# K slots with one kvh per partition quadrant, V in 4-KB runs, one softmax pass for all heads, and P and q turned by VectorE

## Chip, cores, metric

One core of one Trainium2 chip. The time is device microseconds of one execution. It is given as a median with the range over several runs, with the kernel before run again on the same chip each time. A run more than 1.5% above the fastest of its kernel counts as slow.

Some words: a load (DMA) is split into packets, here one for each contiguous run of bytes, which the 16 DMA engines move. A packet lands when its data are written. The tail is the time from the last landing of K or V to the end. The granted clock is the share of its full clock that TensorE was given (1.0 is all). P is the softmax's output, and to turn is to transpose.

## The reference, cut to what matters

Eight decode rows (B = 8, one position each) pass through two rounds of attention (A) and a dense MLP with SiLU (B), with residuals:

```python
x = x + A(layernorm(x), k_cache, v_cache, wq, wo)   # 16 q heads, 8 kv heads, Dh = 256
x = x + B(layernorm(x), w1, w2)
x = x + A(...)      # same weights, same cache
x = x + B(...)
# A: W = 1024; k = k_cache[:, :, Sk-W:, :], v likewise (Sk = 4096);
#    softmax(q k^T / 16) v, each kv head (kvh) serves two q heads
```

The last 1,024 rows of K and V of all 8 batches and 8 kvh are 2 x 33.6 MB in bf16. Both rounds use them, so each batch's K and V stay on chip for both.

## The kernel before, cut to what the change touches

Each batch needs 8 slots for K and 8 for V, each of 128 partitions x 4,096 bytes; 30 slots take turns. SP issues all loads in order, and a load waits until its slot is free. VectorE transposes each K slot in place in 32 x 32 blocks of 4-byte elements. TensorE then takes the scores with q spread over a block-diagonal operand.

```python
def load_k(s, b, kvh):                    # one kvh per slot; 128 x 4,096 B on both sides
    dma(lambda e: e.dma_start(slots[s][:, :].rearrange("p (u d) -> p u d", d=DH),
                              A_k_cache[b, kvh, S0:SK, :].rearrange("(p u) d -> p u d", p=P)), ...)

def load_v(s, b, g):                      # runs of 1,024 B, in the order of P's transpose
    if g >= 4:
        dma(lambda e: e.dma_start(slots[s][:, :].rearrange("v (q n) -> v q n", q=4),
                  A_v_cache[b, g, S0:SK, :].rearrange("(q v uh) d -> v q (uh d)", q=4, uh=2)), ...)
        return
    ...

def softmax(b, layer, prio):              # two halves of four kvh each
    # transpose of the maxima, min, transpose back; then
    for k2 in range(2):
        act(... ACTF.Exp, bias=mb[ei][:, k2:k2 + 1] ...)
    pe([... ident, is_transpose=True ... for c in range(4)], ...)      # P turned by TensorE
    act(... pT_sb ... ACTF.Copy ...)

# q of round 2: a ScalarE copy out of PSUM, then TensorE matmuls turn it
seq = [(b, t, k) for b in range(NB) for t in "kv" for k in range(8)]   # order of the loads
```

## Time and profile before

| | before |
|---|---|
| time | 255.09 us median of 3 (253.25 to 255.13) |
| last packet of K or V lands at | 218.9 us of 255.3 |
| TensorE busy | 195.3 us (76%) |
| chain that ended last | TensorE 59%, SP's queue 16%, DMA 8% |
| median of a 4,096-byte packet | 161 ns |

The row that matters is the second. Until then the 16 DMA engines are busy all the time and pace the batches; after it comes a tail of 36.4 us of compute alone. The profile is of a run of 257.17 us, some 2 us longer than the median; its granted clock dips between 64 and 80 us.

### The profile page before, as it was taken

What the parts mean: (1) busy time and instruction counts of PE and PEld (TensorE: products, weight loads), DVE (VectorE), ACT (ScalarE), POOL (GpSimd) and SP (SyncE); (2) the same over time, 40 slices, a digit from 0 to 9 for tenths busy, and PEclk for the clock granted to TensorE, in tenths of its full rate; (3) what the DMA queues carried; (4) which work ended last, traced back from release to release, by engine and by line L of the source; (5) the groups of instructions that cost most, each with busy time, mean ns of one, the idle gap of its engine ahead of it and who ended that gap; (6) DMA issues with size and microseconds to landing.
All of it is one profiled execution on the core that took longest, in us unless ns stands there. A gap on an engine that the chain in (4) does not pass through costs nothing.

```text
span 255.3 us, 8598 instructions
## 1 busy us (share of the span) xinstructions
PE 195.3 (76%) x3820; PEld 105.1 (41%) x3820; DVE 153.3 (60%) x416; ACT 89.0 (35%) x241; POOL 11.8 (5%) x25
## 2 busy tenths in 40 slices
PE   0053211298869998998899899979988898998795
PEld 0051100043434556454544645444455255443452
DVE  6458665907842895597289559828954685302221
ACT  2002165714213442354343235334432433333211
POOL 1200000000000000000000000000000000000000
PEclk9999999999768999999999999999999899999999
DMA  6999999999999999999999999999999998200000
GB/s 236 361 395 379 309 342 347 352 362 404 369 349 393 372 335 311 392 388 347 362 411 362 338 373 400 350 363 403 372 334 388 379 325 265 75 3 3 0 3 5
DMA packets 50229, 78.23 MB, mean 306 GB/s; under 512 B 2304, under 2 KB 41104, under 8 KB 49808
## 3 DMA queue, kind: packets, MB, share of 16 engines
q1 hardware_dynamic: 50192, 77.68, 87.2%
q8 instruction: 30, 0.49, 0.8%
q14 instruction: 7, 0.06, 0.1%
HBM read 77.67 MB, written 0.01 MB: 304 GB/s over the span
## 4 chain that ended last, share of the span: by engine, by line
PE 59%; SPq 16%; DMA 8%; DVE 6%; ACT 6%; issue 3%; POOL 0%; ACTq 0%; DVEq 0%
PE bank L700 11%; PE bank L641 11%; DMA slot<-in_A_v_cache_dram 8%; PE bank L769 6%; SPq L481 6%; PE bank L817 6%; SPq L431 5%; PE bank L776 5%; ACT qbd L663 3%; PE bank L519 3%; PE bank L804 2%; DVE mseg L648 2%; PE bank L539 2%; SPq L469 2%; ACT qrow L824 2%
## 5 line engine op out<-in xcount | busy, mean ns | idle before, releaser
L946 DVE STREAM_TRANSPOSE slot<-slot 128x512 uint32<-128x512 uint32 x128 | 83.6, 689 | 6.2 <-DMA slot<-in_A_k_cache_dram 5.7
L700 PE MATMUL bank<-slot,pT_sb 128*2 128x256 bf16 x960 | 40.3, 282 | 13.4 <-DMA slot<-in_A_v_cache_dram 10.8
L641 PE MATMUL bank<-slot,qbd 128*8 128x256 bf16 x1024 | 40.7, 298 | 8.7 <-DVE slot L946 6.1
L641 PEld LDWEIGHTS bank<-slot,qbd 128*8 128x8 bf16 x1024 | 26.0, 89 | 15.5 <-DVE slot L946 6.7
L700 PEld LDWEIGHTS bank<-slot,pT_sb 128*2 128x2 bf16 x960 | 19.7, 83 | 24.3 <-issue 10.3
L663 ACT ACTIVATE qbd<-bank,mseg 128x256 bf16<-128x256 f32 x32 | 13.5, 470 | 34.9 <-DVE mseg L659 34.9
L648 DVE TENSOR_REDUCE mseg<-bank 128x1 f32<-128x256 f32 x32 | 13.2, 413 | 19.6 <-PE bank L641 19.3
L714 DVE TENSOR_TENSOR oT<-bank,l_sb 128x16 bf16<-128x16 f32 (+1 forms) x32 | 6.4, 199 | 27.6 <-PE bank L710 26.6
L776 PE MATMUL bank<-wq_sb,cols_b 128*128 128x512 bf16 x64 | 19.6, 388 | 0.0
L754 POOL TENSOR_TENSOR rhalf<-var,nhalf 128x1 f32<-128x1 f32 x16 | 8.8, 549 | 213.7 <-ACT var L752 213.7
L708 ACT ACTIVATE qbd<-bank 128x256 bf16<-128x256 f32 x32 | 12.2, 382 | 18.3 <-PE bank L700 18.3
L769 PE MATMUL bank<-wo_sb,oT 128*1 128x449 bf16 x256 | 17.7, 365 | 0.0
L610 ACT ACTIVATE qbd<-bank,mask 128x128 bf16<-128x128 f32 x32 | 12.1, 378 | 15.6 <-PE bank L605 14.3
L817 PE MATMUL bank<-wq_sb,xbt 128*1 128x512 bf16 x256 | 16.4, 378 | 0.6 <-DVE xbt L743 0.6
L783 PE MATMUL bank<-wq_sb,cols_b 128*128 128x512 bf16 x49 | 14.3, 402 | 0.0
L668 PE MATMUL bank<-ident,qbd 128*128 128x128 bf16 x64 | 6.8, 233 | 9.5 <-ACT qbd L663 8.8
L824 ACT ACTIVATE qrow<-bank 128x512 bf16<-128x512 f32 x16 | 9.5, 596 | 12.3 <-PE bank L817 12.0
L789 ACT ACTIVATE qrow<-bank 128x449 bf16<-128x449 f32 x8 | 4.4, 548 | 21.7 <-PE bank L769 21.7
L450 DVE TENSOR_REDUCE qbd<-wo_sb 128x5 f32<-128x2240 bf16 x4 | 9.7, 2481 | 2.8 <-DMA wo_sb<-in_A_wo_dram 2.8
L624 DVE TENSOR_TENSOR qbd<-bank,maskr 128x256 bf16<-128x256 f32 x16 | 6.8, 424 | 6.2 <-PE bank L619 6.1
L668 PEld LDWEIGHTS bank<-ident,qbd 128*128 128x128 bf16 x64 | 4.0, 103 | 13.6 <-ACT qbd L663 12.8
L710 PEld LDWEIGHTS bank<-ident,qbd 128*128 128x128 bf16 x64 | 3.7, 98 | 12.6 <-ACT qbd L708 6.8
(146 smaller groups left out, 214.9 us busy)
## 6 DMA issues: line engine op xcount, KB each, us to landing
slot<-in_A_k_cache_dram SPq DMA_DIRECT2D x64, 512.0 KB, 8.8
slot<-in_A_v_cache_dram SPq DMA_DIRECT2D x64, 512.0 KB, 8.2
wo_sb<-in_A_wo_dram SPq DMA_DIRECT2D x1, 3584.0 KB, 17.4
wq_sb<-in_A_wq_dram SPq DMA_DIRECT2D x3, 1024.0 KB, 6.8
w_sb<-in_B_w_dram SPq DMA_DIRECT2D x4, 336.0 KB, 15.9
w_sb<-in_B_w_dram SPq DMA_DIRECT2D x1, 1344.0 KB, 11.3
wq_sb<-in_A_wq_dram SPq DMA_DIRECT2D x2, 256.0 KB, 10.0
w_sb<-in_B_w_dram SPq DMA_DIRECT2D x4, 112.0 KB, 9.1
```

Of the source, the lines that this page charges most:

```text
L431: dma(lambda e, j=j: e.dma_start(rows[:, 3 * j:3 * j + 3, :], parts[j, 0:3 * P, :].rearrange("(c p) n -> p c n", p=P)), [("w2", j)], 3 * P ...
L481: dma(lambda e: e.dma_start(slots[s][:, :].rearrange("v (j n) -> v j n", j=4), src.rearrange("j (v uh) d -> v j (uh d)", uh=2)), [("slot", ...
L641: fns.append(lambda e, cb=cb, par=par, j=j, kvh=kvh, kv=kv: e.matmul(bank[sc][32 * j:32 * j + 8, k2 * 256:(k2 + 1) * 256], qbd[qi][:, kvh, ...
L648: dve(lambda e: e.tensor_reduce(mseg[layer][:, k2:k2 + 1], bank[sc][:, k2 * 256:(k2 + 1) * 256], AX.X, ALU.max, negate=True), bk(sc), [("m ...
L663: act(lambda e, k2=k2: e.activation(e_sb[ei][:, k2, :, :].rearrange("p uh (jj ul) -> p uh jj ul", ul=4), bank[sc][:, k2 * 256:(k2 + 1) * 2 ...
L700: fns.append(lambda e, q=q, uh=uh, j=j, vv=vv: e.matmul(bank[ob][32 * j:32 * j + 2, c0:c0 + DH], pT_sb[ei][:, k2 * 2 + uh, j * 8 + 2 * q:j ...
L769: fns.append(lambda e, i=i, c=c, kvh=kvh: e.matmul(bank[XB][32 * c:32 * c + 1, 0:D1], oT1[:, i % 2, i // 2:i // 2 + 1], wo_sb[:, i * DP:i ...
L776: pe([lambda e: e.matmul(bank[SC[1]][:], zero_b.broadcast_to([P, P]), wq_sb[:, 0:512], start=False, stop=True, skip_group_check=True) for ...
L783: pe(lambda e: e.matmul(bank[bi][:], zero_b.broadcast_to([P, P]), wq_sb[:, 0:512], start=False, stop=True, skip_group_check=True), [("wq", ...
L817: pe([lambda e, j=j, c=c, k2=k2, wb=wb: e.matmul(bank[wb][32 * j:32 * j + 1, :], xbt[:, xcol(c, k2):xcol(c, k2) + 1], wq_sb[:, c * HD + (( ...
L824: act(lambda e, wb=wb: e.activation(qrow[:], bank[wb][:], ACTF.Copy), bk(wb), ["rowb"], 0.55, prio, "qrow")
L946: dve(lambda e, v=v: e.transpose(v, v), [("slot", s)], [("slot", s)], 0.67, prio, "KT")
```

## The change

The intent: put four kvh into each K slot, one per quadrant of 32 partitions, so that the scores of all 16 heads of a slot come out of one group of matmuls and the softmax needs one pass. VectorE's 32 x 32 block transpose then turns P, and the keys of P's rows lie so that each V slot is one kvh in runs of 4,096 bytes. The block transpose also turns q of round 2.

```diff
-    def load_k(s, b, kvh):
-        dma(lambda e: e.dma_start(slots[s][:, :].rearrange("p (u d) -> p u d", d=DH),
-                                  A_k_cache[b, kvh, S0:SK, :].rearrange("(p u) d -> p u d", p=P)),
+    def load_k(s, b, i):
+        k2, g = i // 4, i % 4
+        src = A_k_cache[b, 4 * k2:4 * k2 + 4, S0 + 256 * g:S0 + 256 * g + 256, :]
+        dma(lambda e: e.dma_start(slots[s][:, :], src.rearrange("j (i u) d -> j i (u d)", u=8)),
-    def load_v(s, b, g):
-        ... (runs of 1,024 B)
+    def load_v(s, b, kvh):
+        dma(lambda e: e.dma_start(slots[s][:, :], A_v_cache[b, kvh, S0:SK, :].rearrange("(p u) d -> p (u d)", p=P)),
... softmax: two max, two transposes, min -> one max, one scale, one small matmul, one min
-        for k2 in range(2):
-            act(lambda e, k2=k2: e.activation(... ACTF.Exp, bias=mb[ei][:, k2:k2 + 1], scale=1.0),
-        pe([lambda e, c=c: e.matmul(... ident[:, :], is_transpose=True ...) for c in range(4)],
-        act(lambda e: e.activation(pT_sb[ei] ... ACTF.Copy),
+        act(lambda e: e.activation(e_t, bank[sc][:, 0:256], ACTF.Exp, bias=mb[ei][:, 0:1], scale=1.0),
+        dve(lambda e: e.transpose(p_t, e_t), ...)
... q of round 2
-            act(lambda e, wb=wb: e.activation(qrow[:], bank[wb][:], ACTF.Copy),
-            pe([... qturn ...]); dve(... qT2 ...); q_blocks(k2, prio)
+            dve(lambda e, wb=wb: e.transpose(bank[wb][:], bank[wb][:]), ...)
+            dve(... spread straight into qbd ...)
... (q of round 1 spread by GpSimd; tables of the scheduler, which set the order of the work, retuned)
```

## The prediction

> **What bounds the kernel now.** I read the page's slices first, then stretches of 4 us, then the waits and the chain that ended last. The slices:
>
> ```profile
> DMA  6999999999999999999999999999999998200000
> GB/s 236 361 395 379 309 342 347 352 362 404 369 349 393 372 335 311 392 388 347 362 411 362 338 373 400 350 363 403 372 334 388 379 325 265 75 3 3 0 3 5
> DMA packets 50229, 78.23 MB, mean 306 GB/s; under 512 B 2304, under 2 KB 41104, under 8 KB 49808
> ```
>
> The 16 DMA engines are 90% busy or more in nearly all of the first 33 slices (33 x 6.38 = 211 us) and idle afterwards. The rate swings although they are equally busy. Stretches of 4 us in batch 5 and one in the tail show why (columns: length, busy time and instructions of PE, weight load, VectorE, ScalarE, GpSimd, granted clock, DMA share, GB/s):
>
> ```profile
> 152.00:156.00 4.00, 4.00 (x72) 1.81 (x64) 3.72 (x8) 2.93 (x8) 0.55 (x1) 1.00 1.02 412
> 156.00:160.00 4.00, 4.00 (x94) 2.47 (x93) 3.91 (x10) 1.38 (x4) 0.00 (x0) 1.00 1.04 385
> 160.00:164.00 4.00, 3.93 (x72) 1.71 (x74) 3.37 (x8) 1.84 (x5) 0.55 (x1) 1.00 1.09 351
> 164.00:168.00 4.00, 3.29 (x95) 2.44 (x86) 1.82 (x7) 1.12 (x3) 0.00 (x0) 1.00 1.11 348
> 220.00:224.00 4.00, 4.00 (x77) 1.69 (x75) 1.65 (x10) 0.92 (x2) 0.00 (x0) 1.00 0.01 4
> ```
>
> K loads (4,096-byte packets) land at about 407 GB/s, V loads (1,024-byte packets) at about 349. A batch has 8 of each at 524,288 B: 4.19 MB / 407 = 10.3 us and 4.19 / 349 = 12.0 us, together 22.3 us. In the chain the first MLP matmuls of successive batches start at 132.14 and 154.63, a period of 22.5 us. So the middle of the run is DMA-bound; what remains is a tail of about 36 us, from the last V landing near 219 to 255.3, which runs on compute alone. The waits agree:
>
> ```profile
> PE bank L700 <- DMA slot<-in_A_v_cache_dram: 10.8, 7, 4.9
> ```
>
> TensorE loses 10.8 us to late V data, and 5.5 us of that kind stands in the chain in every second batch. Compute alone would need about 22.5 - 2.7 = 19.8 us per batch, close behind the DMA.
>
> **What the Trainium skill says.** "DMA: Bandwidth & Descriptors", section "Why a DMA increments its semaphore by 16 and not by 1": the number k of engines that a DMA uses is the largest one up to 16 that divides the sizes of both access patterns' slowest dimension that is not 1; on the SP queue it is the lowest-numbered k engines, and each adds one semaphore write. The trace agrees. The program has 145 DMAs, of which two (x and the output) have 8 rows: 143 x 16 + 2 x 8 = 2304, and the page counts 2304 packets under 512 B. All of these are 4-byte writes in the packet records. So the 8-row DMAs used 8 engines.
>
> The same page, "Why small descriptors are slow (HBM only)", gives a fixed cost per packet. The packet records agree: median 161 ns for 4,096 B, 48 ns for 1,024 B, 309 ns for 8,192 B. That is 10 ns plus 27.2 bytes per ns. Not one in a hundred of the 4,096-byte packets is under 159 ns, so one engine moves at most 25.7 GB/s.
>
> "SBUF — State Buffer", section "Door 1: The DMA port swizzle": partitions 0..63 reach only the 8 even ports, 64..127 only the odd ones. The trace agrees: among the first 160 packets of 4,096 B lie the 128 of the two 64-partition wq loads. Those 160 took 253 ns in the mean (median 270), the K packets after them 164.
>
> **The change part by part.**
>
> *K loads.* This decides the case. Before, source and destination were both 128 x 2,048, so k = 16. After, as built, the destination is 128 x 2,048 but the source is 4 x 32 x 2,048, the four kvh outermost. The largest k that divides 128 and 4 is 4. All 64 K loads then run on the same four engines, 32 packets of 4,096 B on each, where before it was 8 on each of 16. Load of each of these four engines, at the medians of before:
> - K: 64 x 32 = 2,048 packets x 0.161 = 329.7 us
> - V (one 4,096-byte run per partition, k = 16): 64 x 8 = 512 x 0.161 = 82.4 us
> - weights: 369 x 0.046 (896 B) + 24 x 0.140 + 24 x 0.309 + 8 x 0.075 + 8 x 0.27 = 30.6 us
>
> The sum is 443 us, against roughly 217 us per engine now. None of it lies beside anything that could hide it: compute needs under 20 us per batch, and these four engines need 41.2 + 10.3 = 51.5 us.
>
> *Port conflicts.* Engines 0 and 1 would write partitions 0..31 and 32..63, which share the even ports, and 2 and 3 share the odd ones; each walks through the 8 ports in the same order, four packets on each. In step, a packet would take 270 to 300 ns; more than four packets apart, 161. The four start in step. A few packets per engine in the trace take 0.4 to 1.3 us, and each shifts one engine by some packets, so I estimate that they fall apart within the first 30 to 50 us and then meet by chance. Two engines spread evenly over a cycle of 32 packets conflict for a quarter of it at half strength, +12%; V packets of the other twelve engines cross too. I put K at 0.193 us in the mean (estimate, +20%): 2,048 x 0.193 = 395 us, and the sum at 510 us.
>
> *V loads.* 32,768 packets of 1,024 B become 8,192 of 4,096 B. With K on 16 engines this alone would be 12.0 - 10.3 = 1.7 us per batch, 13.7 us in all. Against it, the first PV group now needs four V slots instead of one.
>
> *Softmax.* Per layer and batch: two maxima, two transposes and one more reduction become one maximum, one scale (about 0.17), one small matmul (0.2) and one reduction (0.16); two Exp become one; four transposing matmuls (0.40) and a ScalarE copy (0.28) become one VectorE transpose of 128x256. From the 512-column transposes (0.689) and the 32-column ones (0.212) I interpolate 0.43. From the last maximum to the first PV the chain shows 237.46 to 240.32 = 2.86 us; I get 2.4, about 0.5 saved.
>
> *q.* The rows that go are these, and the ScalarE copy is on the chain of layer 2:
>
> ```profile
> L824 ACT ACTIVATE qrow<-bank 128x512 bf16<-128x512 f32 x16 | 9.5, 596 | 12.3 <-PE bank L817 12.0
> L624 DVE TENSOR_TENSOR qbd<-bank,maskr 128x256 bf16<-128x256 f32 x16 | 6.8, 424 | 6.2 <-PE bank L619 6.1
> ```
>
> In the tail the chain runs from the first q matmul at 230.50 to the end of scores at 237.43. With a 0.7 us transpose in PSUM and a 0.2 us spread per half, and both q matmul groups back to back, I get 4.1 us: 2.8 saved. Layer-1 spreading moves from ScalarE (12.1 us) to idle GpSimd. VectorE gains 16 x 0.7 and 16 x 0.43 and loses about as much; at 153 us of 255 it has room, and a DMA that feeds it half as fast leaves it more.
>
> *Sum.* Start 2 + DMA 510 + tail 36.4 - 0.5 - 2.8 = 33: 545 us.
>
> **The rivals.**
> 1. K is spread over 16 engines after all. Then all loads run at 407 GB/s, 20.6 us per batch: 255 - 13.7 - 3.3 = 238 us, 7% faster, perhaps 240 to 245 if compute takes over the bound. For it: the change looks meant for that. Against it: the rule and the 2304.
> 2. Four engines without port conflicts: 2 + 443 + 33 = 478 us. For it: nothing holds the engines in step. This is nearly the floor, as 159 ns is the shortest usual packet.
> 3. Four engines in step throughout: K at 0.29 us gives 594 + 113 + 35 = 742 us. Against it: the long packets that shift single engines.
> 4. A wait for four V slots or the doubled VectorE transposes become the bound: a few us, hidden under the K loads.
>
> **Range and chances.** The mechanism rests on a rule whose trace evidence is exact, so I give it 94%. Within it the open size is the conflict: 478 without, 742 with it always. I take 545, and 468 to 680 as the range. Faster 5% (rival 1), the same 1%, slower 94%.
>
> **What would show each step right or wrong.** Right: packets under 512 B fall to 79 x 16 + 64 x 4 + 2 x 8 = 1536; mean rate near 78 / 0.545 = 143 GB/s; DMA digits of 3 to 5 instead of 9; K issue to landing tens of us instead of 8.8; VectorE's transposes wait for K loads, and PE's busy share falls below 45%. The packet records tell the conflict apart: the median of 4,096 B stays 161 to 165 with a tail near 300, or lies at 270 and more. Wrong: 2304 small packets, DMA at 9 throughout and 400 GB/s in V stretches as well, which is rival 1. The softmax and q steps can only be seen in the tail, as 33 against 36 us after the last V landing.

## The result, and the profile after

524.48 us median of 4 (523.06 to 525.66), against 255.11 (253.25 to 259.39) for the kernel before. The ratio is 2.061, 95% interval 2.048 to 2.074. The 259.39 counts as slow. Here and below a ratio is the one for the fast runs (here the means, 524.42 over 254.49), so not quite the ratio of the quoted medians.

The page of the kernel after: TensorE's busy time, then its slices and those of the DMA, and the packets.

```profile
PE 231.2 (44%) x3601; PEld 108.9 (21%) x3628; DVE 160.4 (31%) x404; ACT 60.0 (11%) x162; POOL 16.5 (3%) x41
PE   0201108250272338531764067333853176423988
DMA  7224995239422654247422933275423942284200
GB/s 285 99 104 140 270 370 221 100 117 238 139 104 104 194 155 156 103 146 201 160 105 105 231 132 138 105 181 159 161 103 129 216 159 98 104 200 140 99 1 4
DMA packets 24882, 78.19 MB, mean 150 GB/s; under 512 B 1536, under 2 KB 7568, under 8 KB 24464
```

Packets under 512 B fell from 2304 to exactly the 1536 that four engines per K load imply. The DMA digit is no longer 9 but swings between 2 and 9, and where it is 2 (two tenths of 16 engines) the rate is 98 to 105 GB/s. Stretches of 6 us of the same run (columns as in the prediction's table of stretches):

```profile
386.00:392.00 6.00, 4.53 (x44) 1.31 (x45) 1.84 (x5) 1.46 (x4) 0.55 (x1) 0.54 0.26 104
404.00:410.00 6.00, 0.00 (x0) 0.00 (x0) 1.30 (x2) 0.00 (x0) 0.00 (x0) 0.60 1.03 246
410.00:416.00 6.00, 0.00 (x0) 0.00 (x0) 0.00 (x0) 0.00 (x0) 0.00 (x0) 0.50 1.02 232
440.00:446.00 6.00, 3.54 (x45) 1.43 (x48) 1.54 (x3) 1.14 (x3) 0.13 (x1) 0.50 0.26 104
494.00:500.00 6.00, 5.58 (x101) 2.49 (x99) 0.79 (x5) 2.01 (x5) 0.55 (x1) 1.00 0.01 3
```

Three kinds of stretch: four engines alone (share 0.26, 104 GB/s, so 26 GB/s each); all 16 busy but only 232 to 246 GB/s, with every compute engine nearly idle; and the tail. The packet records say the same. For 287 us of the run about four packets are in flight, and a 4,096-byte one takes 163.6 ns in the mean. For 140 us at least 15 are in flight, and one takes 249 ns in the mean (median 268). The last packet of V lands at 490.0 us, and the tail is 33.0 us.

The waits of VectorE's K transposes, first of the kernel before, then of the kernel after (us in total, times, longest):

```profile
DVE slot L946 <- DMA slot<-in_A_k_cache_dram: 5.7, 4, 4.0
```

```profile
DVE slot L909 <- DMA slot<-in_A_k_cache_dram: 286.6, 64, 8.1
```

Before, 4 waits for K; after, 64 and 286.6 us. The wait for K now ends the chain too. The chain by engine, before and after, and three pieces of the chain after (start, us, what):

```profile
PE 59%; SPq 16%; DMA 8%; DVE 6%; ACT 6%; issue 3%; POOL 0%; ACTq 0%; DVEq 0%
```

```profile
DMA 53%; SPq 27%; PE 12%; DVE 5%; issue 2%; ACT 0%; ACTq 0%
...
391.66 29.65 DMA slot<-in_A_k_cache_dram
...
427.37 16.21 DMA slot<-in_A_k_cache_dram
...
449.67 30.22 DMA slot<-in_A_k_cache_dram
```

Each batch of the second half has one such pair, about 45 us of K that nothing hides. The granted TensorE clock fell as well (mean 0.739 against 0.973), but TensorE is 44% busy and in the tail, where it does bound, the clock is back at 1.0.

### The profile page after: what moved, and what is told of

Its sections match the earlier page's. It is cut to its first block, busy times and chain, and to the rows that moved or that the text cites. A ratio compares the mean times of both kernels' runs of the same rounds, so it can differ in the third digit from the quotient of the medians.

```text
span 523.0 us, 8141 instructions
## 1 busy us (share of the span) xinstructions
PE 231.2 (44%) x3601; PEld 108.9 (21%) x3628; DVE 160.4 (31%) x404; ACT 60.0 (11%) x162; POOL 16.5 (3%) x41
## 2 busy tenths in 40 slices
DMA packets 24882, 78.19 MB, mean 150 GB/s; under 512 B 1536, under 2 KB 7568, under 8 KB 24464
## 4 chain that ended last, share of the span: by engine, by line
DMA 53%; SPq 27%; PE 12%; DVE 5%; issue 2%; ACT 0%; ACTq 0%
DMA slot<-in_A_k_cache_dram 53%; SPq L475 14%; SPq L479 8%; SPq L435 3%; DVE slot L909 3%; PE bank L631 3%; PE bank L672 2%; PE bank L516 2%; PE bank L742 1%; PE bank L749 1%; DVE bank L791 1%; SPq L424 0%; PE bank L783 0%; PE bank L715 0%; PE bank L805 0%
## 5 line engine op out<-in xcount | busy, mean ns | idle before, releaser
L909 DVE STREAM_TRANSPOSE slot<-slot 128x512 uint32<-128x512 uint32 x128 | 86.4, 696 | 286.8 <-DMA slot<-in_A_k_cache_dram 286.6
L631 PE MATMUL bank<-slot,qbd 128*16 128x256 bf16 x1024 | 53.0, 376 | 97.6 <-DVE slot L909 45.8
L783 PE MATMUL bank<-wq_sb,xbt 128*1 128x512 bf16 x256 | 28.2, 584 | 100.7 <-DVE xbt L709 98.3
L631 PEld LDWEIGHTS bank<-slot,qbd 128*16 128x16 bf16 x1024 | 29.8, 114 | 125.2 <-DVE slot L909 47.5
L672 PE MATMUL bank<-slot,ep 128*2 128x256 bf16 x960 | 43.3, 302 | 12.8 <-DMA slot<-in_A_v_cache_dram 11.1
L672 PEld LDWEIGHTS bank<-slot,ep 128*2 128x2 bf16 x960 | 20.2, 85 | 28.6 <-issue 21.7
L677 ACT ACTIVATE ep<-bank 128x256 bf16<-128x256 f32 x32 | 12.3, 383 | 27.8 <-PE bank L672 25.8
L770 PE MATMUL bank<-w_sb,hT 128*1 128x449 bf16 x112 | 12.8, 551 | 2.7 <-DVE hT L767 2.7
L516 PE MATMUL bank<-w_sb,xbt 128*1 128x448 bf16 x128 | 11.8, 512 | 0.0
L791 DVE STREAM_TRANSPOSE bank<-bank 128x512 f32<-128x512 f32 x16 | 11.1, 694 | 1.2 <-PE bank L783 1.2
L454 DVE TENSOR_REDUCE ep<-wo_sb 128x5 f32<-128x2240 bf16 x4 | 9.7, 2479 | 4.0 <-DMA wo_sb<-in_A_wo_dram 4.0
L683 DVE TENSOR_TENSOR oT<-bank,l_sb 128x16 bf16<-128x16 f32 (+1 forms) x32 | 6.1, 190 | 14.5 <-PE bank L679 14.4
```

Source lines behind the costliest of these rows:

```text
L516: pe([lambda e, c=c, j=j: e.matmul(bank[XB][32 * j:32 * j + 1, 0:D], xbt[:, xcol(c, j // 2):xcol(c, j // 2) + 1], w1_r(j, c), start=(c == ...
L631: fns.append(lambda e, cb=cb, par=par, g=g, kv=kv: e.matmul(bank[sc][32 * g:32 * g + H, 0:256], qbd[qi][:, k2, cb * 2 + par, :], kv[:, cb, ...
L672: fns.append(lambda e, u=u, j=j, vv=vv, pt=pt: e.matmul(bank[ob][32 * j:32 * j + 2, c0:c0 + DH], pt, vv, start=(u == 0), stop=(u == 7), ti ...
L783: pe([lambda e, j=j, c=c, k2=k2, wb=wb: e.matmul(bank[wb][32 * j:32 * j + 1, :], xbt[:, xcol(c, k2):xcol(c, k2) + 1], wq_sb[:, c * HD + (( ...
L791: dve(lambda e, wb=wb: e.transpose(bank[wb][:], bank[wb][:]), bk(wb), bk(wb), 0.74, prio, "qT")
L909: dve(lambda e, v=v: e.transpose(v, v), [("slot", s)], [("slot", s)], 0.67, prio, "KT")
```

## The experiments

Ten kernels. Those that read wrong K or V rows are wrong; the comparison with the reference passed all of them all the same, so it is too coarse to see which rows are read, and does not prove the others right either. Medians and ranges are over all runs; slow were one of two in runs 2 and 7, one of six in run 6, and two of four in runs 8, 9 and 10.

**1. One kvh per K load again (a_k16; wrong).** Only the source of K changes.

```diff
-        src = A_k_cache[b, 4 * k2:4 * k2 + 4, ...]; ... src.rearrange("j (i u) d -> j i (u d)", u=8)
+        ... A_k_cache[b, i, S0:SK, :].rearrange("(p u) d -> p (u d)", p=P)
```

> The changed kernel with each K load reading one kvh as 128 rows of 4 KB, as the kernel before does (wrong result on purpose; every instruction on the other engines and all bytes stay). Theory (K loads confined to four engines are the whole loss): packets under 512 B back at 2304, all 16 engines busy, 238 us, 232 to 246. Rival (the softmax, the q turn or the V loads cost something themselves): the loss stays in part, over 260 us. Rival (the compute chain is now the bound): 240 to 250 with the DMA row below 9 in the middle.

Measured: 240.69 us (238.94 to 241.49, 4 runs); ratio 0.946 (0.938 to 0.954). Its page:

```profile
DMA  5999999999999999999999999999999999300000
GB/s 223 383 372 398 303 338 370 409 396 374 407 406 411 407 407 395 410 387 405 356 409 352 409 378 384 403 392 407 394 396 355 409 363 401 136 3 3 0 6 3
DMA packets 25650, 78.19 MB, mean 329 GB/s; under 512 B 2304, under 2 KB 8336, under 8 KB 25232
```

2304 small packets are back, the DMA is at 9 throughout, and V stretches run at 400 GB/s and more like K's. The view of one source is the whole loss, and the rest of the change is worth 5%.

**2. Eight kvh per K load (a_k8; wrong).** The source is 8 x 16 x 2,048, so eight engines.

```diff
-        src = A_k_cache[b, 4 * k2:4 * k2 + 4, S0 + 256 * g:S0 + 256 * g + 256, :]
+        src = A_k_cache[b, :, S0 + 128 * i:S0 + 128 * i + 128, :]
```

> The changed kernel with K loads whose source has 8 kvh outermost and 128 rows of each (8 x 16 x 2,048 elements; wrong result on purpose). Theory (engines = largest divisor of the outermost sizes): 8 engines, packets under 512 B = 79 x 16 + 64 x 8 + 2 x 8 = 1792; per engine 1,024 K packets x 0.162 = 166 us, V 82, weights 31, together 279 us plus the slow stretches seen while V loads run (45 us in the changed kernel, perhaps half of that here), plus 2 and 33: 315 to 360 us. Rival (any source with a short outermost dimension is equally slow, or the distance of 2 MB between rows is what costs): about 520 us, as in the changed kernel.

Measured: 380.08 us (377.21 to 382.94, 2 runs, the second slow), above the range expected.

```profile
GB/s 301 181 186 210 275 350 415 218 225 235 205 203 226 230 189 215 208 233 204 224 185 226 203 235 183 229 215 226 225 231 217 201 246 228 215 202 134 2 2 3
DMA packets 25138, 78.19 MB, mean 209 GB/s; under 512 B 1792, under 2 KB 7824, under 8 KB 24720
```

1792 = 79 x 16 + 64 x 8 + 2 x 8: the count of engines follows the source's outermost size. After the first seven slices and up to the tail the row shows little but 183 to 246 GB/s. In the packet records the stretches with 15 or more packets in flight last 152 us, at 252 ns per packet (median 276), as in the changed kernel. With about eight in flight it is 176 ns and not the 162 expected, so some of the excess lies there too.

**3. The four blocks close together (a_k4near; wrong).** Still 4 x 32 x 2,048, but the blocks lie 132 KB apart in one kvh and not 2 MB apart. This asks whether the distance in HBM matters: the Trainium skill, "DMA: Bandwidth & Descriptors", section "Latency and other measured facts", reports lower rates for copies between HBM tensors with row pitches of large powers of two (164 GB/s at 2 MiB against 207 at 512 KiB).

```diff
+        src = A_k_cache[b, i, S0 - 64:S0 + 992, :].rearrange("(j r) d -> j r d", j=4)[:, 0:256, :]
```

> The changed kernel with K loads of the same shape 4 x 32 x 2,048 but the four blocks 132 KB apart inside one kvh instead of 2 MB apart in four (wrong result on purpose). Theory (engine count, set by shape alone): 515 to 530 us, 1536 small packets. Rival A (the 2 MB distance in HBM makes K slow): back to 240 to 300 us. Rival B for the 45 us above the floor (the 2 MB distance makes K and V disturb each other while both run): about 480 us, with the 4,096-byte packets of the busy stretches back near 161 ns instead of 268.

Measured: 522.75 us (521.48 to 524.02, 2 runs); ratio 2.055 (2.035 to 2.075). The full stretches have 247 ns per packet (median 269), the four-engine ones 164. Here the distance explains neither the loss nor the slow full stretches.

**4. The kernel before with only the new K load (b_k4; wrong).**

```diff
     def load_k(s, b, kvh):
+        k2, g = kvh // 4, kvh % 4
+        src = A_k_cache[b, 4 * k2:4 * k2 + 4, S0 + 256 * g:S0 + 256 * g + 256, :]
+        ... src.rearrange("j (i u) d -> j i (u d)", u=8)
```

> The kernel before with only the K load given the new shape (4 kvh x 256 rows per slot; wrong result on purpose), V in 1 KB runs, softmax and q as before. Theory: K 330 us + V 2,048 packets x 0.048 = 98 us + weights 31 = 459 us per engine, plus 2, tail 36 and 30 to 60 us of disturbance: 525 to 560 us. Rival (the new softmax or q part is needed for the loss): under 300 us.

Measured: 518.67 us (516.47 to 520.86, 2 runs); ratio 2.039 (2.018 to 2.060).

```profile
DMA packets 49461, 78.23 MB, mean 151 GB/s; under 512 B 1536, under 2 KB 40336, under 8 KB 49040
```

One edit makes the old kernel as slow as the new. The last packet of V lands at 480.5 us and the tail is 38.5 us, so the new V and softmax give nothing back here: they save 5.5 us in the tail, but with 4-KB V runs the last packet lands 9.5 us later.

**5. The kernel before with only V in 4-KB runs (b_v4k; wrong).**

```diff
-        ... (both forms of the V load, 1,024-B runs)
+        dma(lambda e: e.dma_start(slots[s][:, :], A_v_cache[b, g, S0:SK, :].rearrange("(p u) d -> p (u d)", p=P)),
```

> The kernel before with V loaded as one kvh per slot in 4 KB runs and nothing else changed (wrong result on purpose, same schedule). Theory (the middle is DMA-bound, V runs are worth 1.7 us per batch): 241 us, 239 to 245, last V landing near 206 instead of 219, tail still 36 us. Rival (compute sets the period as soon as the DMA is faster): 246 to 252 us.

Measured: 251.72 us (250.28 to 253.16, 6 runs) against 254.88; ratio 0.990 (0.986 to 0.995). My theory fell, its rival held: the last V landed at 216.1 us and not near 206. The row of the main DMA queue (packets, MB, share of 16 engines' span), before and in this run, with TensorE's wait for V in this run, and in both the longest of SP's waits for TensorE before a load:

```profile
q1 hardware_dynamic: 50192, 77.68, 87.2%
...
SPq L475 <- PE bank L827: 27.6, 7, 5.9
```

```profile
q1 hardware_dynamic: 25616, 77.68, 82.9%
...
PE bank L692 <- DMA slot<-in_A_v_cache_dram: 7.1, 4, 5.1
...
SPq L474 <- PE bank L819: 36.2, 6, 6.5
```

DMA work fell from 0.872 x 255.3 = 222.6 us to 0.829 x 250.9 = 208.0, about the 13.7 us that I had worked out. Only 3 of them show in the time: the share of busy DMA fell in place of the span. TensorE's wait for V went from 10.8 to 7.1 us, but VectorE's for K rose from 5.7 to 9.8, and all of SP's waits for TensorE before loads rose from 89.8 to 105.3 us, by about as much as the DMA had saved. The first MLP matmuls of successive batches (second to last batch) came every 22.9 us, before every 23.0. So the loads now wait for compute to free their slots, and bytes alone no longer set the pace. The chain that ended last would not show this: there the DMA's share rose from 8% to 17%.

**6. The a_k16 kernel with V back in 1-KB runs (a_k16_v1k; wrong).** This leaves the new softmax and q alone, with the retuned tables and GpSimd's spread of q that belong to them.

```diff
-        ... A_v_cache[b, kvh, S0:SK, :].rearrange("(p u) d -> p (u d)", p=P)
+        ... (the two forms of the kernel before)
```

> The variant with K on 16 engines, with V put back to the 1 KB runs of the kernel before (wrong result on purpose), so that softmax and q are what is new against the kernel before. Theory (they shorten only what runs on compute alone): DMA end back at 219, tail 31 to 33 instead of 36, 250 to 252 us. Rival (they also take time out of each batch): under 248. Rival (they are worth nothing): 254 to 256.

Measured: 250.62 us (249.15 to 253.0, 6 runs); ratio 0.988 (0.982 to 0.993), as expected; the last V lands at 215.5 us (219 expected), the tail is 31.5 us.

```profile
q1 hardware_dynamic: 50192, 77.68, 90.3%
...
PE bank L678 <- DMA slot<-in_A_v_cache_dram: 21.3, 9, 11.2
```

Here it is the reverse: less compute, and TensorE waits 21.3 us for V where it waited 10.8, and SP's waits for TensorE fall from 89.8 to 69.6 us. V runs alone give 1.0%, softmax and q alone 1.2% (both under the 2% that a verdict asks for, but clear of noise), both together 5.4%. Each part meets the other limit just behind the one that it moves. The order of the work differs between the two kernels too, and no run separates what that gives.

**7. Sixteen engines, each on eight neighbouring partitions (a_k16s; wrong).** The source is 16 x 8 x 2,048, the kvh of two batches; the blocks lie 2 MB apart.

```diff
+        b0, r0 = b - b % 2, S0 + 64 * (i + 8 * (b % 2))
+        src = A_k_cache[b0:b0 + 2, :, r0:r0 + 64, :]
+        ... src.rearrange("b j (i u) d -> (b j) i (u d)", u=8)
```

> The changed kernel with K loads of 16 x 8 x 2,048 elements, 16 kvh of two batches outermost: 16 engines, but each with 8 partitions in a row[...] (wrong result on purpose). Theory (packets slow down to about 268 ns when more engines run than have ports of their own): K at 220 to 260 GB/s, 285 to 310 us, 2304 small packets. Rival (the slow stretches come from something else, or the engines fall out of step as the four did): 238 to 250 us, 4,096-byte packets at 161.

Measured: 298.28 us (295.64 to 300.93, 2 runs, the second slow).

```profile
DMA  6999999999999999999999999999999999950000
GB/s 263 315 249 247 291 342 391 412 263 255 280 408 250 259 307 352 241 226 308 374 240 243 298 396 233 248 318 361 255 264 356 323 245 253 364 219 4 0 2 4
DMA packets 25650, 78.19 MB, mean 267 GB/s; under 512 B 2304, under 2 KB 8336, under 8 KB 25232
```

2304 small packets, so all 16 engines work and are busy, yet slices of K run at 226 to 263 GB/s while slices of V in the same run reach 412. So the number of engines is not all. The edit moves the partitions of each engine, and with them the distance between the engines' rows in HBM, which run 3 cleared for four engines only; run 8 is without that distance.

**8. Each K load as four loads of one quadrant (a_kquad; correct).** The data land as in the changed kernel, but both sides of each load are 32 x 2,048, so k = 16.

```diff
+        def part(j):
+            src = A_k_cache[b, 4 * k2 + j, S0 + 256 * g:S0 + 256 * g + 256, :]
+            return lambda e: e.dma_start(slots[s][32 * j:32 * j + 32, :], src.rearrange("(i u) d -> i (u d)", u=8))
+        dma([part(j) for j in (0, 2, 1, 3)], ...)         # each adds 16 to the slot's semaphore
```

> The changed kernel with each K load cut into four loads of one kvh and 32 partitions each, in the order quadrant 0, 2, 1, 3 (correct result). Each uses 16 engines, two partitions each, on the 8 ports of one half. Theory with port sharing: K at 220 to 260 GB/s, 285 to 315 us, so no repair that beats the kernel before. If the engines fall out of step: 240 to 247 us, a repair that beats it. Small packets: 79 x 16 + 256 x 16 + 2 x 8 = 5376.

Measured: 289.86 us (285.62 to 291.21, 4 runs); ratio 1.131 (1.122 to 1.140). It takes back most of the loss, but it is still slower than before. Stretches in the first K, the first V and a later K:

```profile
22.00:26.00 4.00, 0.21 (x2) 0.13 (x2) 2.93 (x6) 0.00 (x0) 0.00 (x0) 1.00 1.03 253
50.00:54.00 4.00, 1.32 (x28) 0.89 (x32) 4.00 (x2) 2.96 (x12) 0.00 (x0) 1.00 1.03 410
98.00:102.00 4.00, 3.50 (x47) 1.37 (x43) 2.68 (x6) 1.46 (x3) 0.19 (x1) 1.00 1.05 282
```

The engines are as busy in K as in V (shares of 1.03 to 1.05) and move 253 against 410 GB/s: in K a packet takes 260 ns, in V 163. Each load reads 128 KB in one piece here, so the distance in HBM is not needed for slow K; smaller and more numerous loads are this run's own rival.

**9. The quadrant loads with a skew between neighbouring engines (a_kskew; correct).** Dummy loads on 1, 3, 5, ... 15 engines before the first K load put every even engine one 8,192-byte packet behind its odd neighbour, to see whether neighbours in step slow each other.

```diff
+    for k in range(1, 16, 2):
+        p0 = (k // 2) ** 2
+        dma(lambda e, k=k, p0=p0: e.dma_start(wo_sb[p0:p0 + k, 0:4096],
+            A_v_cache[0, 0, 0:16 * k, :].rearrange("(k r) d -> k (r d)", k=k)), ...)
```

> The quadrant loads (a_kquad, 289.9 us, correct) with nothing changed but a skew at the start: before the first K load, eight dummy loads of one 8,192-byte packet per engine on k = 1, 3, 5, ... 15 engines, so that in every pair of neighbouring engines the even one is one such packet (0.31 us, two K packets) behind the odd one. [...]Theory (the slow K stretches are neighbours in step on one port, and the lag holds while the engines never run dry): K stretches at 161 to 175 ns and 380 to 400 GB/s, time 243 to 258, which would be a correct kernel no slower than before and perhaps faster. Rival 1: the lag is lost at the first stretch in which the queues run dry (batch changes, waits for V slots): early batches fast, later ones slow again, 265 to 285. Rival 2: the slow stretches have nothing to do with which engine meets which on a port: 290 to 294, since the dummy loads cost engine 0 2.5 us.

Measured: 287.92 us (283.99 to 289.71, 4 runs), no clear gain (fast runs 283.99 and 287.49, in run 8 285.62 and 289.39). The same three stretches:

```profile
22.00:26.00 4.00, 0.21 (x2) 0.13 (x2) 3.23 (x5) 0.00 (x0) 0.00 (x0) 1.00 1.03 326
50.00:54.00 4.00, 0.00 (x0) 0.00 (x0) 3.43 (x2) 3.34 (x11) 0.00 (x0) 1.00 1.02 408
98.00:102.00 4.00, 3.44 (x66) 1.93 (x69) 2.87 (x6) 1.34 (x4) 0.55 (x1) 1.00 1.04 287
```

The first K runs at 326 in place of 253 GB/s (packets of 202 ns in place of 260), steadily from 20 to 28 us, and V is as it was, so who is in step with whom matters. But the gain was never the whole difference, and by 98 us it is gone. The dummy loads cost time as well: from 14 to 18 us the DMA moves 154 GB/s, in run 8 250. Nearest is the first rival, that the lag is lost; the theory's 243 to 258 us fell. That the trace does not name engines leaves the lag itself unseen.

**10. K loads of the changed kernel issued by GpSimd (a_kpool; correct).** The Trainium skill, "DMA: Bandwidth & Descriptors", section "Why a DMA increments its semaphore by 16 and not by 1", says that loads issued from GpSimd with k under 16 take k consecutive engines from a round-robin cursor; it also names copies from there that get 16 engines all the same. Run 10 asks whether K spreads over all 16.

```diff
-        self.order["sp"] = loads
+        self.order["sp"] = [t for t in loads if t.name != "kload"]
+        self.order["pool"] = sorted(self.order["pool"] + [K loads], key=lambda t: (t.start, t.idx))
```

> The changed kernel with its correct K loads untouched (source 4 x 32 x 2,048, so four engines each), but issued from GpSimd's queue in place of SP's; the Trainium skill says that such transfers take k consecutive engines from a round-robin cursor and not always the lowest k. Theory: four loads in flight then cover all 16 engines, and the work per engine falls from 443 us to about 210; with no port conflicts the time is near the 240.7 of the one-kvh source, with conflicts like those of the 16 x 8 source and of the quadrant loads (221 to 230 ns per packet) 270 to 300; GpSimd's issuing time and its two waits in the MLP chain may add some us. Predicted 250 to 295. Rival 1: the same four engines are taken whatever the queue: about 524. Rival 2: GpSimd needs so long for each issue that K comes late: PE waits for K, the DMA row below 9, over 300. Signs: the DMA row in tenths, the concurrency of 4,096-byte packets and their mean, the count of packets under 512 B (2304 if all 16 engines post for each such load).

Measured: 542.13 us (533.59 to 554.52, 4 runs; the two fast ones 533.59 and 540.42). From its page, and two of its waits:

```profile
DMA packets 50226, 78.29 MB, mean 145 GB/s; under 512 B 26880, under 2 KB 32912, under 8 KB 49808
## 3 DMA queue, kind: packets, MB, share of 16 engines
q0 software_dynamic: 33792, 33.66, 47.1%
q1 hardware_dynamic: 16400, 44.13, 37.6%
...
DVE slot L914 <- DMA slot<-in_A_k_cache_dram: 265.0, 39, 21.0
...
POOL slot L479 <- PE bank L677: 124.0, 6, 26.7
```

The theory's 250 to 295 us fell. The second rival's "over 300" holds as a number but not as a cause: an issue takes GpSimd 0.69 us, 44 us for all 64. At least 14 packets were in flight for 403 us of the run, so the loads do not queue one packet at a time on four engines. But a K packet took 448 ns in the mean, and where K runs alone with 14 and more in flight it moves only about 51 packets per 2 us, 105 GB/s in the mean, no more than the four engines alone moved in the changed kernel. There are also 24,576 more 4-byte packets than K's 16 completions per load explain; the 4-byte packets of this queue take only 15 ns each. 24,576 is 64 loads x 12 x 32, as if each load had sent 32 to each of twelve other engines; that is arithmetic and not shown. My own rearrangement adds a wait of unknown cost: GpSimd stands 124 us at K loads for their slots, and works in order, so its part of the MLP waits behind them. Whether the loads went to different engines and met on the same ports, or to the same four, this run does not tell.

## Why the prediction was right, and where its steps were not

- **K on four engines: right, exactly.** 1536 small packets, 104 GB/s in K stretches, and 2304 and 240.7 us with nothing but the source undone (run 1); the same loss from this one edit in the old kernel (run 4).
- **The floor of 443 us: consistent.** The four engines alone run at 163.6 ns per 4,096-byte packet where I took 161.
- **Port conflicts: the wrong place, and too large.** This is the step that failed. I put +20% on K for conflicts among the four K engines, 67 us over the floor, with 30 to 50 us until they fall out of step. Measured: the DMA ends at 490, so 490 - 2 - 443 = 45 us over it. Among the four there is next to nothing. They did start slow, at 229 to 270 ns between 13 and 14.5 us with about five packets in flight, but from 17 us on it is 161: if this is the falling apart that I had in mind, it took about 5 us and not 30 to 50. The 45 us lie where all 16 engines are busy: 7,355 packets of 4,096 B in those stretches at 249 instead of 161 ns, over 16 engines, are 40 us (a mean over the engines, which the records do not name). The four-engine stretches add (163.6 - 161) ns x 7,379 / 4 = 5 us. By the order of the queues these are the stretches with K on four engines and V on the other twelve. I had named that crossing in half a sentence and gave it no number of its own. It is also part of what made eight engines slower than expected (run 2).
- **What slows the full stretches is not settled.** The distance between the blocks in HBM is out (run 3). For 16-engine loads, that the step between engines matters is shown (run 9). That the partitions an engine writes matter fits runs 7 and 8 both, while the rivals (distance in HBM, small loads) fit only one each. That K and V on different engines slow each other in the same way is argued only.
- **V runs: right as DMA work (14.6 us less), wrong as time.** Alone they gave 3 us (run 5). I had put compute at 19.8 us per batch by subtracting TensorE's named V waits from the period; what failed is the step that compute could follow at that pace. The period stayed at 22.9 us, and the time saved went into SP's waits for TensorE. In the change as intended, with K on 16 engines, the V runs do give 10 us (250.6 to 240.7).
- **Softmax and q: right.** The tail went from 36.4 to 33.0 us, as the prediction had it, and 1.2% alone (run 6) is 3 us. The tails of all profiles agree: 34.9 to 38.5 us with the old compute, 31.5 to 33.2 with the new. Once V is in 4-KB runs they give more, 11 us (251.7 to 240.7), presumably because compute then holds the batches as well.
- **Rival 1: its mechanism did not happen, its number holds.** It gave 238, perhaps 240 to 245, for K on 16 engines; run 1 has 240.7.
- **Sum.** 545 predicted, 524.5 measured, 20.5 too many. The conflict term alone was 22 too large (67 against 45); the rest of the sum is within 2 us. Of the 67, 1.7 are a slip: 395 + 82 + 31 is 508, not 510. That the total came out within 4% is partly luck: the 67 us were put where about 5 were lost, and the 40 in the full stretches had no number of their own.

No correct version beats the kernel before. The layout asks for the kvh outermost over the partitions, and the loads tried that keep it cost 290 (quadrants), 288 (skewed) or 542 us (GpSimd).

## What to carry to other kernels

Before a layout that packs several blocks into one load, look at the outermost size of both sides of the transfer and count engines: one source view here cost more than everything else in the change together, and the count of 4-byte packets proved it in one line. Then look at which partitions each engine gets, since other ways to use 16 engines cost about 47 to 55 us again (fast runs of 8 and 7 against run 1). And where DMA and compute lie as close as here, price two improvements together, not one by one: here 1.0% and 1.2% made 5.4%.

## What the Trainium skill lacked or had wrong

- "DMA: Bandwidth & Descriptors", "Why a DMA increments its semaphore by 16 and not by 1": the rule for k held exactly (2304, 1792 and 1536 small packets for 16, 8 and 4). It lacks what a load on few engines does to full-width loads beside it: 232 to 246 GB/s over all 16 engines and 249 ns per packet, where either kind alone has 161 to 164 ns. That these stretches are the two kinds together is inferred from the order of the queues.
- Same page, "Rules for kernel authors": a multiple of 16 outermost is not enough. With k = 16 on both, 16 x 8 partitions took 298 us and quadrants of 32 took 290, against 241 for 128 rows of one block. For the quadrants "SBUF — State Buffer", "Door 1: The DMA port swizzle", does give a warning, as 32 partitions reach only 8 of 16 ports; for 16 x 8 I found none.
- Same section as the first: the round-robin of GpSimd's loads brought no relief (542 us, 448 ns per K packet), and I found nothing on the page that accounts for 24,576 additional 4-byte packets in 64 such loads.
- "DMA: Bandwidth & Descriptors", "Where 436 GB/s comes from": it says that for transfers between HBM and SBUF the limit of about 358 GB/s of HBM binds. With one core running, whole slices here reach 405 to 411 GB/s (run 1), so that sentence needs a condition; the page's own single-core table under "Bandwidth" goes above 358 too.
